# Turning z by overlapping twos of tiles, sixteen buffers of squares, shared homes for turned blocks and a changed plan, in a gated attention and token mixing kernel

## The chip, the cores and the metric

The kernel runs on one core of one Trainium2 chip. Its time is the device time of one execution in microseconds; lower is better. The figure for a kernel is the median of several runs. A profiled execution also has a span, from the first to the last instruction on the core; the device time holds that and a little around it.

## What is computed

There are 8 batches of 3200 tokens; u and v have 256 columns, z has 64. First a gated attention without a softmax, then a token mixer on its result:

```python
scores = scale * np.matmul(z, z.transpose(0, 2, 1))      # 3200 x 3200, symmetric
attn = np.maximum(scores, 0.0) ** 2
x = u * np.matmul(attn, v)

wq, wk = x @ w_q, x @ w_k                                # 64 columns each
W_tok = scale * np.einsum('bsd,btd->bst', wq, wk)
mixed = np.einsum('bst,btd->bsd', W_tok, x)
out = np.maximum(mixed, 0.0) @ w_out
```

The mixer is linear up to the maximum, so the kernel forms wk-transposed times x first (the "heads", 64 x 256) and never holds W_tok.

## The kernel before, in words

**Tiles and groups.** The 3200 tokens of a batch are 25 tiles of 128 rows. The columns of the score matrix are taken in 7 groups: six of 512 columns (four tiles) and one of 128. For a group `gi`, the product of the squared scores with v needs all 25 tiles of rows. Scores are symmetric, so a block of squares that was made in one group can be turned (transposed, by a DMA on SP's queue) and used in a later one: `is_turned` (L212) says that group `gi` makes for `gj` up to two groups further on (`FAR`, L45), and for the last group. So group 0 makes 25 tiles itself, group 1 makes 21, groups 2 to 5 make 17 each and the last one 1. Two such tiles make a pair; there are 460 or so pairs in all.

**A pair.** `scores` (L242) makes two tiles of scores on TensorE, with z turned (columns on partitions) as both operands. z has 64 columns, so the turned z of a batch, `zT`, holds it twice, on partitions 0 to 63 and on 64 to 127. One tile of the pair uses the top half of TensorE's rows, the other the bottom half, and the two run side by side. `first_stage` (L262) takes the maximum with zero and a scale out of PSUM, on ScalarE or VectorE. `second_stage` (L279) squares, on ScalarE or GpSimd, into an fp16 buffer `at` of the pool `pat` (`NAT`, 14 buffers, L52), and asks for the turning of what later groups need (`turn`, L304, into tiles `tt1`, `tt2` by the distance of the groups, or `ttl` for the last group).

**The second product.** `second_product` (L326) multiplies a tile of squares with v into four PSUM accumulators, two halves of the group by two halves of the rows; a group of 512 columns takes 100 steps of two matmuls. `gate` (L342) adds the two row halves (ScalarE copies, VectorE adds) and multiplies by u on GpSimd, which gives x in a buffer of `px` (`NX`, 6). x is turned by DMA (`turn_x`, L380, pool `pxt`, 3), projected to queries and keys (`projections`, L397), the keys are turned back and doubled (`turn_keys`, L416, `double_keys`, L426), and `heads` (L433) accumulates keys times x. When a batch's heads are known, `mix` (L462) and `proj` (L485) make the output rows, which SP stores.

**z of later batches.** `load_z` (L154) brings a batch's z in fp16 into a tile `zn` by a DMA of GpSimd's queue. `double_z` (L158) copies it twice by VectorE into `zd`, so that each token has its 64 values two times side by side. `turn_z` (L163) turns it in five DMAs of five tiles. Each turned block of 128 columns then has the same 64 values on the top and on the bottom partitions. z of the first batch is turned by TensorE instead (`turn_first`, L122), out of a buffer `zd0`.

**The order of the work.** The whole program is unrolled, and its order is written out by a planner that runs when the kernel is built (L556 to L997). It keeps a clock for each of TensorE, VectorE, ScalarE and GpSimd, adds a fixed cost for each instruction that it issues (`give`, L560), and holds lists of what may begin when: `later` (things at a time), `extras` (projections, heads, mixes, outputs), and `moves` (DMAs of SP, each with a time from which it is ready, a due time, an issue cost and a transfer cost; `move`, L581, `send`, L584). A transfer counts as landed `LANDS` (4.0) us after its cost. `row_at` tells from when a tile of squares may be used. The main loop (L963) takes, at each point of TensorE's clock, an extra, a pair of scores or a step of the second product. A pair counts as wanted when it stands in an even share of all pairs to all steps, 140 steps ahead (`lead`, L961); it can only be made when the pair `NAT` before it is used up and its turnings have landed:

```python
        wanted = able and p * total < (done_acc + lead) * NPAIR
```

What runs on the chip is the order that comes out; the engines wait for each other by semaphores, not by the planner's clock.

Of the kernel before, what the change touches and what calls it, by code (L numbers as in the profile page):

```python
# [16 lines left out]
def kernel(  # L17
# [34 lines left out]
    NAT = 14  # L52
    NX = 6
# [9 lines left out]
    pxt = ctx.enter_context(tc.tile_pool(name="pxt", bufs=3))  # L63
# [23 lines left out]
    zT, vs, us, xs, xTs, qks, ks, hacc, hss, rts, zds = ({} for _ in range(11))  # L87
# [64 lines left out]
    zdense, ztimes = {}, []  # L152

    def load_z(b):  # L154
        zdense[b] = pz.tile([P, NT, dqk], FP16, tag="zn", name="zn")
        nc.gpsimd.dma_start(out=zdense[b][:], in_=rows(z, b))

    def double_z(b, half):  # L158
        if half == 0:
            zds[b] = pz.tile([P, NT, 2, dqk], FP16, tag="zd", name="zd")  # L160
        nc.vector.tensor_copy(out=zds[b][:, :, half, :], in_=zdense[b][:])

    def turn_z(b, i):  # L163
        ztimes.append((b, i))
        if i == 0:
            zT[b] = pzt.tile([P, S], FP16, tag="zT2", name="zT2")
# [12 lines left out]
    wq32 = consts.tile([P, NC, dh], FP32, tag="wq32", name="wq32")  # L179
    wk32 = consts.tile([P, NC, dh], FP32, tag="wk32", name="wk32")  # L180
# [29 lines left out]
    SKIP = [(0, 2)]  # L210

    def is_turned(b, gi, gj):  # L212
        if b == 0 and (gi, gj) in SKIP:
            return False
        return gi < gj and (gj <= gi + FAR or gj == LASTG)
# [24 lines left out]
    made, turned = {}, {}  # L240

    def scores(p):  # L242
        assert len(ztimes) >= 5 * tiles[2 * p + 1][0] and p_chunk(p) in z_at, (p, clock, len(ztimes), z_at)
        sc = ps_tile("sc")
        for h, (b, gi, ti) in enumerate(tiles[2 * p : 2 * p + 2]):
# [3 lines left out]
                lhsT=zT[b][top(h), ts(ti, P)],  # L249
                rhs=zT[b][top(h), ds(gs, gw)],  # L250
# [28 lines left out]
    def second_stage(p, g, ways):  # L279
# [24 lines left out]
        def turn(b, gi, gj, n0, nn, c0, c1):  # L304
            if (b, gi, gj) not in turned:
                kind, nr, bufs = ("l", 1, 8) if gj == LASTG else (gj - gi, 4, gj - gi + 2)
                turned[b, gi, gj] = ptt.tile(
                    [P, nr, 4, P], FP16, tag=f"tt{kind}", name=f"tt{kind}", bufs=bufs
                )
# [32 lines left out]
    def gate(b, gi, half):  # L342
# [9 lines left out]
        if b == last and gi >= LASTG - 2:  # L352
            if gi == LASTG - 2 and half == 0:
                spare = pz.tile([P, NT, 2, dqk], FP16, tag="zd", name="xd")
                spare = spare[:].rearrange("p n a k -> p (n a k)")
                spare = spare[:, 0 : 9 * D].rearrange("p (n d) -> p n d", d=D)
# [23 lines left out]
    def turn_x(b, gi):  # L380
        assert len(xTs) < 3
# [192 lines left out]
    LANDS = 4.0  # L574
# [45 lines left out]

    SPLIT = 0.2
# [28 lines left out]
    def squares():  # L650
        while pending and pending[0][0] <= clock[PE] + 0.3:
# [9 lines left out]
            for (b, gi, gj, _, nn, _, _), turn in second_stage(p, g, ways):  # L661
                n = nn * widths[gi] // P
                due = done + (4.0 if gj == gi + 1 else 9.0)
                out_of[p] = out_of.get(p, 0) + 1
                move(done + SLACK, due + SLACK, 1.28, 0.21 * n, turn, lambda t, x=(p, b, gi, gj, nn): block_landed(t, *x))
# [17 lines left out]
    def use_keys(b, gi):  # L683
# [15 lines left out]
        if not final:  # L699
            move(  # L700
                done + SLACK, done + 10.0, 1.28, 0.21 * n, lambda: turn_keys(b, gi),
                lambda t: at_time(t, lambda: double(b, gi)),
            )
            keyed.append((b, gi))
# [46 lines left out]
    def use_proj(b, gi):  # L751
# [13 lines left out]
        move(done + SLACK, done + 6.0, 0.55, 1.6, stores[0], landed)  # L765
# [5 lines left out]
    Z0 = 24  # L771
    V0 = 56
    V1 = 11

    def batch_begun(b, t):
        if b + 1 < B:
            t0 = max(t + 6, Z0)
            at_time(t0, lambda: (load_z(b + 1), push(3.0)))
            for half in range(2):
                at_time(  # L780
                    t0 + 12 + 3 * half,
# [316 lines left out]
```

## Time and profile before

| | before |
|---|---|
| median of three runs | 784.41 us |
| the three runs | 782.69, 784.41 and 789.05 us |
| profiled execution | 784.44 us |
| its span | 782.7 us |
| granted TensorE clock | 0.999 |
| read from and written to HBM | 59.64 and 26.21 MB |

The profile gives, for each engine, the time in which it executed something (busy) and how many instructions that were. PE is TensorE with its matmuls, PEld its weight loads, DVE VectorE, ACT ScalarE, POOL GpSimd and SP the queue that issues most DMAs. "L332" is a line of the kernel. `acc` is the second product, `sc` the scores, `g` the result of the first stage, `at` the squares, `tt` and `ttl` turned blocks, `both` the sum of the row halves, `x_sb` x, `kx` the keys, `qk` queries and keys, `mx` and `fo` the output stage.

### The profile page before, as it was taken

What the parts mean: (1) busy time and instruction counts of PE and PEld (TensorE: products, weight loads), DVE (VectorE), ACT (ScalarE), POOL (GpSimd) and SP (SyncE); (2) the same over time, 40 slices, a digit from 0 to 9 for tenths busy, and PEclk for the clock granted to TensorE, in tenths of its full rate; (3) what the DMA queues carried; (4) which work ended last, traced back from release to release, by engine and by line L of the source; (5) the groups of instructions that cost most, each with busy time, mean ns of one, the idle gap of its engine ahead of it and who ended that gap; (6) DMA issues with size and microseconds to landing.
All of it is one profiled execution on the core that took longest, in us unless ns stands there. A gap on an engine that the chain in (4) does not pass through costs nothing.

```text
span 782.7 us, 28343 instructions
## 1 busy us (share of the span) xinstructions
PE 769.8 (98%) x12410; PEld 663.7 (85%) x12410; DVE 503.3 (64%) x515; ACT 546.4 (70%) x663; POOL 645.1 (82%) x530
## 2 busy tenths in 40 slices
PE   7999999999999999999999999999999999999996
PEld 5899999788899878888889887998889888898784
DVE  6766556655587556786476665777567556566635
ACT  6868777668676767766677767776678676777534
POOL 7898988788889877888789889778788879888961
PEclk9999999999999999999999999999999999999999
DMA  7999999999999999999799989999999998969635
GB/s 179 143 174 170 157 181 180 165 175 206 216 174 177 211 184 189 185 212 189 180 177 174 220 173 201 168 164 217 190 188 152 183 228 166 202 127 210 142 59 213
DMA packets 306300, 140.88 MB, mean 180 GB/s; under 512 B 285056, under 2 KB 287744, under 8 KB 306176
## 3 DMA queue, kind: packets, MB, share of 16 engines
q1 hardware_dynamic: 299408, 122.90, 82.1%
q0 software_dynamic: 6624, 15.98, 15.0%
q8 instruction: 97, 1.59, 0.9%
q10 hardware_dynamic: 144, 0.20, 0.1%
q14 instruction: 27, 0.22, 0.1%
HBM read 59.64 MB, written 26.21 MB: 110 GB/s over the span
## 4 chain that ended last, share of the span: by engine, by line
PE 92%; DVE 2%; DMA 1%; ACT 1%; POOL 1%; issue 1%; DVEq 0%; SPq 0%; ACTq 0%
PE acc L332 67%; PE sc L247 13%; PE fo L493 6%; PE qk L401 3%; PE qk L438 2%; PE mx L466 1%; DVE g L273 1%; DMA v_sb<-in_v_dram 1%; POOL at L291 1%; ACT g L269 1%; ACT at L289 0%; DMA z<-in_z_dram 0%; DVE fo L516 0%; PE hd L438 0%; DVE both L349 0%
## 5 line engine op out<-in xcount | busy, mean ns | idle before, releaser
L291 POOL TENSOR_TENSOR at<-g 128x1024 f16<-128x1024 f32 (+2 forms) x252 | 457.1, 1827 | 62.4 <-DVE g L273 50.3
L332 PE MATMUL acc<-v_sb,at 64*128 64x256 f16 x7344 | 498.4, 269 | 1.2 <-DMA v_sb<-in_v_dram 0.7
L273 DVE TENSOR_SCALAR g<-sc 128x1024 f32<-128x1024 f32 (+2 forms) x320 | 372.6, 1178 | 135.3 <-PE sc L247 126.7
L332 PEld LDWEIGHTS <-at 64*128 64x128 f16 x7344 | 400.9, 94 | 55.2 <-issue 8.1
L289 ACT ACTIVATE at<-g 128x1024 f16<-128x1024 f32 (+2 forms) x230 | 228.1, 1008 | 19.2 <-DVE g L273 17.0
L269 ACT ACTIVATE g<-sc 128x1024 f32<-128x1024 f32 (+2 forms) x159 | 156.5, 986 | 67.1 <-PE sc L247 58.5
L247 PE MATMUL sc<-zT 64*128 64x512 f16 x924 | 187.6, 377 | 1.9 <-DVE g L273 0.8
L370 POOL TENSOR_TENSOR x_sb<-both,u_sb 128x512 f16<-128x512 f32 (+1 forms) x112 | 134.7, 1209 | 43.9 <-DVE both L349 43.6
L332 PE MATMUL acc<-v_sb,tt 64*128 64x256 f16 x2272 | 159.2, 269 | 0.0
L332 PEld LDWEIGHTS <-tt 64*128 64x128 f16 x2272 | 123.5, 94 | 14.3
L349 DVE TENSOR_TENSOR both<-acc,both 128x512 f32<-128x512 f32 (+1 forms) x104 | 69.7, 670 | 86.4 <-ACT both L348 73.3
L348 ACT COPY both<-acc 128x512 f32<-128x512 f32 (+1 forms) x104 | 59.0, 568 | 70.7 <-PE acc L332 66.4
L247 PEld LDWEIGHTS <-zT 64*128 64x128 f16 x924 | 60.8, 94 | 12.9 <-issue 8.9
L521 ACT ACTIVATE fo<-fo 128x1024 f32<-128x1024 f32 (+1 forms) x48 | 44.6, 930 | 24.3 <-PE fo L493 23.8
L493 PE MATMUL fo<-wo,rt 128*128 128x256 f16 x400 | 53.2, 274 | 1.3 <-ACT rt L481 0.5
L483 ACT ACTIVATE rt<-mx 128x1024 f16<-128x1024 f32 (+1 forms) x49 | 45.6, 934 | 11.5 <-PE mx L466 11.2
L414 ACT CAST qk<-qk 128x512 f16<-128x512 f32 (+1 forms) x54 | 29.4, 544 | 30.0 <-PE qk L438 24.1
L493 PEld LDWEIGHTS <-rt 128*128 128x128 f16 x400 | 34.9, 98 | 15.8 <-issue 10.9
L453 DVE TENSOR_TENSOR ha<-qk,ha 128x512 f32<-128x512 f32 x37 | 25.6, 691 | 30.7 <-ACT qk L414 30.2
L401 PE MATMUL qk<-xT_sb,wqk 64*128 64x256 f16 (+1 forms) x404 | 32.4, 265 | 0.0
L431 POOL COPY kx<-kx 128x128 f16<-128x128 f16 (+1 forms) x99 | 26.2, 294 | 5.7 <-DMA kx<-qk 5.7
L438 PE MATMUL qk<-x_sb,kx 64*128 64x256 f16 x342 | 28.4, 269 | 0.0
(45 smaller groups left out, 233.7 us busy)
## 6 DMA issues: line engine op xcount, KB each, us to landing
u_sb<-in_u_dram SPq DMA_DIRECT2D x48, 512.0 KB, 4.9
out_dram<-fo SPq DMA_DIRECT2D x47, 512.0 KB, 5.2
v_sb<-in_v_dram POOLq DMA_DIRECT2D x35, 320.0 KB, 5.5
zn<-in_z_dram POOLq DMA_DIRECT2D x7, 400.0 KB, 6.8
tt<-at SPq DMA_TRANSPOSE x143, 4.3
u_sb<-in_u_dram SPq DMA_DIRECT2D x8, 128.0 KB, 3.1
out_dram<-fo SPq DMA_DIRECT2D x8, 128.0 KB, 3.4
xT_sb<-x_sb SPq DMA_TRANSPOSE x56, 5.8
```

What stands on the lines that cost most here:

```text
L247: nc.tensor.matmul(out=sc[:, h, 0:gw], lhsT=zT[b][top(h), ts(ti, P)], rhs=zT[b][top(h), ds(gs, gw)], start=True, stop=True,)
L269: nc.scalar.activation(out=g[:, hs, 0:w], in_=sc[:, hs, 0:w], func=RELU, scale=GSCALE)
L273: nc.vector.tensor_scalar(out=g[:, hs, 0:w], in0=sc[:, hs, 0:w], scalar1=0.0, scalar2=GSCALE, op0=AOP.max, op1=AOP.mult,)
L289: nc.scalar.square(out=out, in_=g[:, hs, 0:w])
L291: nc.gpsimd.tensor_mul(out=out, in0=g[:, hs, 0:w], in1=g[:, hs, 0:w])
L332: nc.tensor.matmul(out=accs[half, r][:, ds((j % 2) * D, D)], lhsT=weights(b, gi, ti, j)[top(r), :], rhs=vs[b][top(r), ti, :], start=(first ...
L348: nc.scalar.copy(out=both[:, 0 : n * D], in_=accs[half, 0][:, 0 : n * D])
L349: nc.vector.tensor_add(out=both[:, 0 : n * D], in0=accs[half, 1][:, 0 : n * D], in1=both[:, 0 : n * D])
L370: nc.gpsimd.tensor_mul(out=xs[b, gi][:, 0:n, :, r, :].rearrange("p n c d -> p (n c) d"), in0=both[:, 0 : n * D].rearrange("p (m d) -> p m ...
L401: nc.tensor.matmul(out=ps[:, r, 0 : n * P], lhsT=wqk[top(r), c, :, :].rearrange("p t h -> p (t h)"), rhs=xTs[b, gi][top(r), 0:n, c, :], st ...
L483: nc.scalar.activation(out=out, in_=ps[:, 0:nr, 0 : ND * n * P], func=RELU)
L493: nc.tensor.matmul(out=banks[r][:, ds(j * D, D)], lhsT=flat[:, ds((dc * n + j) * P, P)], rhs=wo[:, dc, :], start=(dc == 0 and j == 0), sto ...
```

## The change

- **z turned by overlapping twos of tiles.** `double_z` and its copies go, and with them `zd`. One tile `zn` holds all 25 tiles of z with one column of zeros (64 values) before and one behind. A turning takes two neighbouring tiles side by side as one block of 128 columns: block k of the turned z has tile k − 1 on the top partitions and tile k on the bottom ones. So `zT` is one block longer (26), and the top half is read 128 columns further on (`z_cols`), except for the first batch, which TensorE turns as before. The blocks are turned in four DMAs, even and odd ones apart, of 7, 7, 6 and 6 blocks, instead of five of 5.
- **Buffers.** 16 for squares (14), 7 for x (6), 4 for turned x (3). `zd0` and the spare tile of the last batch use buffers of v, the fp32 query and key weights use a buffer of the output stage.
- **Shared homes for turned blocks.** The seven buffers of `tt1` (3) and `tt2` (4) become seven homes for any block. A home is taken when the first turning of a block is sent and given back when the second product has used all rows of the block; a turning for which there is no home stays in the planner's list.
- **Pairs by need.** Each pair gets the step at which its own group wants it, spread evenly over that group's steps, and is wanted 140 steps ahead of it.
- **The plan's figures.** `LANDS` 8.0 (4.0), the cost of a turned block 0.17 (0.21), of rows of u or of the output 1.3 (1.6), of loads of z and v 2.2 and 1.8 (3.0 and 2.5); turnings for the last group from three groups off are due after 12 (9); the projections come 7 us after x has landed (3); z is turned from 14 us after its load on, in steps of 7 us (5 in the first batch), where it was 18 us and 6 (4).

`EXTRA` is empty and `STRETCH` is 1.0, so neither changes anything. The diff, cut to its core:

```diff
-    NAT = 14
-    NX = 6
+    NAT = 16
+    NX = 7
+    NXT = 4
...
-    zd0 = pz.tile([P, NT, 2, dqk], FP16, tag="zd", name="zd")
+    zd0 = pv.tile([P, NT, 2, dqk], FP16, tag="v_sb", name="zd")
...
-    zT[0] = pzt.tile([P, S], FP16, tag="zT2", name="zT2")
+    zT[0] = pzt.tile([P, S + P], FP16, tag="zT2", name="zT2")
+    zn = pz.tile([P, NT + 2, dqk], FP16, tag="zn", name="zn")
...
+    ZTURNS = [(0, 0, 7), (1, 0, 7), (0, 7, 13), (1, 7, 13)]
...
-    def double_z(b, half):
-        if half == 0:
-            zds[b] = pz.tile([P, NT, 2, dqk], FP16, tag="zd", name="zd")
-        nc.vector.tensor_copy(out=zds[b][:, :, half, :], in_=zdense[b][:])
...
         nc.sync.dma_start_transpose(
-            out=zT[b][:].rearrange("p (n s) -> p n s", s=P)[:, 5 * i : 5 * i + 5, :],
-            in_=zds[b][:, 5 * i : 5 * i + 5, :, :].rearrange("p n a k -> p (n a k)"),
+            out=zT[b][:].rearrange("p (m o s) -> p o m s", o=2, s=P)[:, odd, m0:m1, :],
+            in_=zn[:, 2 * m0 + odd : 2 * m1 + odd, :].rearrange("p n k -> p (n k)"),
         )
+
+    def z_cols(b, h, at, n):
+        return zT[b][top(h), ds(at + (P if b and h == 0 else 0), n)]
...
+    NHOME = 7
+    homes, homes_free = {}, list(range(NHOME))
+
+    def has_home(b, gi, gj):
+        return gj == LASTG or (b, gi, gj) in turned or bool(homes_free)
+
+    def give_home_back(b, gj, t):
+        gi = group_of(t)
+        if (b, gi, gj) in homes and all(
+            (b, gj, starts[gi] // P + n) in used for n in range(widths[gi] // P)
+        ):
+            homes_free.append(homes.pop((b, gi, gj)))
...
-                due = done + (4.0 if gj == gi + 1 else 9.0)
+                due = done + {1: 4.0, 2: 9.0}.get(gj - gi, FARDUE)
...
+                    lambda x=(b, gi, gj): has_home(*x),
...
-    LANDS = 4.0
+    LANDS = 8.0
+    BLOCK = 0.17
+    ROWS4 = 1.3
...
-    XWAIT = 3.0
+    XWAIT = 7.0
...
+    for p in range(NPAIR):
+        b, gi, _ = tiles[2 * p]
+        i0, i1 = first_of[b, gi], ends[b, gi]
+        n = NT * (widths[gi] // P)
+        need.append(steps[b, gi] + STRETCH * n * (2 * p - i0) / (i1 - i0))
...
-        wanted = able and p * total < (done_acc + lead) * NPAIR
+        wanted = able and need[p] < done_acc + lead
```

More of the change, by code (lines that the diff above doesn't have):

```diff
@@ L305, in turn @@
             if (b, gi, gj) not in turned:
[L306 to L309, printed above, removed]
+                if gj == LASTG:
+                    tag, nr, bufs = "ttl", 1, 8
+                else:
+                    homes[b, gi, gj] = home = homes_free.pop(0)
+                    tag, nr, bufs = f"tt{home}", 4, 1
+                turned[b, gi, gj] = ptt.tile([P, nr, 4, P], FP16, tag=tag, name=tag, bufs=bufs)
             out = turned[b, gi, gj][:].rearrange("p n j t -> p (n j) t")
@@ L777, in batch_begun @@
             t0 = max(t + 6, Z0)
[L778 to L781, printed above, removed]
-                    lambda half=half: (double_z(b + 1, half), give(DVE, clock[PE], 0.98)),
-                )
-            step = 6 if b else 4
-            for i in range(5):
+            if b == 0:
+                nc.gpsimd.memset(zn[:, 0 : NT + 2 : NT + 1, :], 0.0)
+            at_time(t0, lambda: (load_z(b + 1), push(2.2)))
+            step = ZSTEP if b else ZSTEP0
+            for i, (_, m0, m1) in enumerate(ZTURNS):
                 move(
-                    t0 + 18 + step * i, t0 + 34 + step * i, 1.28, 1.05,
+                    t0 + ZWAIT + step * i, t0 + ZDUE + step * i, 1.28, BLOCK * (m1 - m0),
                     lambda i=i: turn_z(b + 1, i),
@@ L903, in acc_step @@
         used.add(row)
+        if row:
+            give_home_back(*row)
         if closes:
@@ L961 @@
     lead = 140
+    STRETCH = 1.0
+    need, at, seen = [], 0, 0
+    steps = {}
+    for b in range(B):
+        for gi in range(NG):
+            steps[b, gi] = at
+            at += NT * (widths[gi] // P)
+    first_of = {}
+    for i, (b, gi, t) in enumerate(tiles):
+        first_of.setdefault((b, gi), i)
+    for p in range(NPAIR):
[3 more added lines that the diff above has]
+        need.append(steps[b, gi] + STRETCH * n * (2 * p - i0) / (i1 - i0))
     turn_about = False
```

57 lines of the change are left out of this document (32 added, 25 removed).

## The prediction

> **What bounds the kernel now.** I read the page's busy times first, then the chain that ended last, then busy times by stage, then who TensorE waited for.
>
> ```profile
> span 782.7 us, 28343 instructions
> PE 769.8 (98%) x12410; PEld 663.7 (85%) x12410; DVE 503.3 (64%) x515; ACT 546.4 (70%) x663; POOL 645.1 (82%) x530
> PE 92%; DVE 2%; DMA 1%; ACT 1%; POOL 1%; issue 1%; DVEq 0%; SPq 0%; ACTq 0%
> ```
>
> TensorE is busy for 98% and carries 92% of the chain. A busy TensorE need not be at its peak, because its matmuls overlap, so the pace has to be seen. The second view is the chain in order of time (start, us, what); its one long line is that of the stretch from 160 to 400 us alone.
>
> ```profile
> by line: PE acc L332 71.9%; PE sc L247 13.7%; PE fo L493 6.9%; PE qk L401 3.1%; PE qk L438 2.7%; PE mx L466 1.5%; PE hd L438 0.4%
> 252.45 1.85 PE fo L493 x16
> 254.95 1.86 PE acc L332 x34
> 740.76 0.22 PE sc L247 x2
> 747.84 11.79 PE acc L332 x214
> ```
>
> From 160 to 400 us the chain never leaves TensorE. The step of the second product takes 1.86/34 = 54.7 ns a matmul there, and 11.79/214 = 55.1 ns near the end, where there is nothing left but this step. So the pace is the same in the full kernel and with all other work gone: this is TensorE's own rate. Two matmuls run side by side, so a matmul shown as 269 ns long begins every 54.7 ns. Next, busy times by stage (stretch, its length, then TensorE matmuls, weight loads, VectorE, ScalarE, GpSimd with counts, granted clock, DMA share, GB/s):
>
> ```profile
> 0.00:20.00 20.00, 15.84 (x192) 11.88 (x194) 13.20 (x18) 12.28 (x20) 14.82 (x22) 1.00 0.75 177
> 20.00:40.00 20.00, 19.25 (x310) 16.61 (x308) 15.36 (x16) 16.71 (x22) 16.86 (x13) 1.00 0.93 142
> 40.00:60.00 20.00, 19.72 (x330) 18.19 (x327) 13.02 (x14) 14.21 (x18) 18.78 (x17) 1.00 1.12 179
> 80.00:120.00 40.00, 40.00 (x684) 38.85 (x682) 22.99 (x24) 31.41 (x40) 37.81 (x33) 1.00 1.20 161
> 120.00:140.00 20.00, 19.14 (x323) 17.12 (x321) 11.91 (x14) 14.54 (x17) 16.77 (x15) 1.00 1.00 173
> 160.00:760.00 600.00, 599.77 (x9774) 514.40 (x9770) 388.29 (x393) 417.56 (x498) 504.18 (x407) 1.00 0.98 183
> 760.00:783.00 23.00, 16.09 (x168) 11.19 (x163) 12.35 (x16) 9.91 (x19) 3.77 (x4) 0.97 0.49 183
> ```
>
> In 600 of the 782.7 us TensorE idles for 0.23 us. What idles is the start (4.16 us in the first 20), 0.75, 0.28 and 0.86 us in three stretches up to 140 us, and the end (22.7 − 16.09 = 6.6 us). What it waited for, by releaser (us in total, times, longest):
>
> ```profile
> PE hd L438 <- POOL kx L431: 0.9, 1, 0.9
> PE sc L247 <- DVE g L273: 0.8, 3, 0.4
> PE sc L247 <- ACT g L269: 0.8, 3, 0.3
> PE acc L332 <- DMA v_sb<-in_v_dram: 0.7, 1, 0.7
> PE acc L332 <- DVE both L349: 0.4, 2, 0.2
> ```
>
> Two rows for sizes below, a group of instructions (busy us, mean ns of one, idle before) and a step of the chain:
>
> ```profile
> L332 PE MATMUL acc<-v_sb,at 64*128 64x256 f16 x7344 | 498.4, 269 | 1.2 <-DMA v_sb<-in_v_dram 0.7 <-DVE both L349 0.4
> 138.51 0.28 PE hd L438 x2
> ```
>
> No row names a turned block, a turned z or a square's buffer. The changed kernel has the same number of matmuls in each product, so only these waits can give anything. The visible idle time from 20 to 760 us is 0.75 + 0.28 + 0.86 + 0.23 = 2.1 us. A gap shows short by up to 269 − 109 = 160 ns, because the last matmul before it is still running; with some eight gaps that is at most 1.3 us more: 3.4 us is all there is to gain there.
>
> The Trainium skill (Perfetto Trace Analysis, Identifying the Most-Contended Engine) says that matmul busy time is a poor measure of distance to the roofline and that the busy share of weight loads is a good one. By it, 85% would leave 119 us of headroom, and a change that hides waits could win far more than 1%. The equal paces above disagree: the weight loads are fewer per microsecond only where a matmul streams 512 columns.
>
> **The change part by part.** Counts of instructions in the changed kernel are from the order in which the two built programs hold them; no time is in it. Durations (groups first; then single instructions: start, us; then transfers: count and median us to landing) are these:
>
> ```profile
> L291 POOL TENSOR_TENSOR at<-g 128x1024 f16<-128x1024 f32 (+2 forms) x252 | 457.1, 1827 | 62.4 <-DVE g L273 50.3
> L273 DVE TENSOR_SCALAR g<-sc 128x1024 f32<-128x1024 f32 (+2 forms) x320 | 372.6, 1178 | 135.3 <-PE sc L247 126.7
> L289 ACT ACTIVATE at<-g 128x1024 f16<-128x1024 f32 (+2 forms) x230 | 228.1, 1008 | 19.2 <-DVE g L273 17.0
> L269 ACT ACTIVATE g<-sc 128x1024 f32<-128x1024 f32 (+2 forms) x159 | 156.5, 986 | 67.1 <-PE sc L247 58.5
> L161 DVE COPY zd<-zn 128x1600 f16<-128x1600 f16 x14 | 13.7, 975 | 0.0
> L291 POOL TENSOR_TENSOR at<-g 128x1024 f16<-128x1024 f32 x234 | 440.5, 1895 | 60.1 <-DVE g L273 48.5 <-issue 3.7 <-ACT g L269 3.0
> 40.04 0.97 DVE L161 COPY zd<-zn 128x1600 f16<-128x1600 f16 x1
> 310.83 1.91 POOL L291 TENSOR_TENSOR at<-g 128x1024 f16<-128x1024 f32 x1
> 311.32 0.98 DVE L161 COPY zd<-zn 128x1600 f16<-128x1600 f16 x1
> tt<-at SPq DMA_TRANSPOSE x143, 4.3
> zT<-zd SPq DMA_TRANSPOSE x35, 4.8
> ```
>
> *z without copies.* 14 copies of 975 ns leave VectorE: 13.7 us, none of it on the chain from 160 us on. The planner fills the room: 18 first stages move from ScalarE to VectorE and 18 squares from GpSimd to ScalarE. That is about +18 × 1.18 − 13.7 = +7.5 us on VectorE, +18 × (1.01 − 0.99) = +0.4 us on ScalarE, −18 × 1.895 = −34 us on GpSimd. All three stay below TensorE, so the cost and the gain are nothing beyond the waits above. Seven turnings of z per later batch in fives become four issues in sevens and sixes: 28 issues on SP for 35, 26 blocks a batch for 25. At 4.8 us for five blocks the extra block costs under 1 us of DMA per batch. What hides it: turned z is first read at a batch's end, and no row of TensorE waits names it; without that cover each issue would cost its 4.8 us. The two zero columns are one small memset on GpSimd's queue ahead of its first square, which waits there for its input anyway.
>
> The Trainium skill (SBUF — State Buffer, SBUF: two separate sides) says that a two-port VectorE copy locks GpSimd out of the shared port for its whole length. By it the 14 copies, the first at 40.04 us in the stretch where TensorE lost 0.28 us, would hold GpSimd for 13.7 us, and their removal could take that 0.28 us too: 782.8 us for my sum below. The trace disagrees: the square from 310.83 us runs beside the copy from 311.32 us and takes 1.91 us against a mean of 1.895 for its form, so I give nothing for it.
>
> *Sixteen buffers and pairs by need.* Pairs are now made ahead of the group that wants them instead of at an even rate. In matmuls of TensorE's order, the median distance from a pair's scores to the first use of its squares rises from 147 to 190 (5th percentile 93 to 89, least 67 to 53). At 54.7 ns, 147 matmuls are 8 us, 53 are 2.9 us, against about 1.2 + 1.8 us for the two stages by VectorE and GpSimd. So the typical cover grows, and the thinnest places are no safer than before.
>
> *Homes and late landings.* 141 two-tile turnings stand on SP as before. From the last scores that feed a turned block to its first use the median goes from 621 to 715 matmuls, 34 to 39 us, against 4.3 us for the transfer; the least is 313 matmuls (17 us), in the first batch. A transfer held back for a home waits in the planner's list, not on SP, so nothing queues behind it. Planning a landing at 8 instead of 4 us makes rows come into use later: this is the cover that grows. Nothing on TensorE waits for this now, so it brings nothing by itself; it removes a risk.
>
> *Buffers of x and turned x, shared weights and a spare.* Seven for six, four for three, three tiles moved into others' buffers: no instruction more. XWAIT of 7 moves the projections later, and the next batch's heads with them; no one waits for these at the seams, except once (0.9 us for `kx` at 138.5 us). The kernel's last stretch has the same instructions in nearly the same order.
>
> *What is added on TensorE.* 9 heads join a projection's tile instead of a tile of their own, but projections of the output stand alone two times more: 114 changes between 64-row and 128-row matmuls for 110. The row of 16 such matmuls takes 1.85 us, 16 × 109.4 ns would be 1.75, so a change costs about 0.1 us: +0.4 us. From below the bound is 0, if two changes of a visit cost it once, +0.2.
>
> *Sum.* The profiled execution took 784.44 us, its span 782.7, so 1.74 us lie around it; the median of the three runs is 784.41 (782.69 to 789.05). The waits from 20 to 760 us, 3.4 us at most, I take as half gone, because the order of the work is new from about 26 us on and brings waits of its own: −1.7. The changes of shape: +0.4. The start and the end, 4.16 + 6.6 us, keep their orders: 0. 784.44 − 1.7 + 0.4 = 783.1 us. Ends: all of the waits gone and shape changes at +0.2, 781.2; none gone, and as much again added, 784.44 + 3.4 + 0.4 = 788.2.
>
> **The rivals.**
>
> *The waits only move (no effect).* The rows allow it: they are few, each is a meeting of particular instructions, and the thinnest distances did not grow. 784.44 + 0.4 = 784.8 us.
>
> *Pairs by need crowd the first group of each batch (slower).* A pair costs (372.6 + 156.5 + 457.1 + 228.1)/462 = 2.63 us on three engines. Group 0 has 12.5 pairs in 100 steps of two matmuls, against 9.2 at an even rate. Its TensorE time is 200 × 0.0547 + 25 × 0.11 = 13.7 us and, with 1 to 2 us of heads and projections, some 15: 45 us on three engines. The pairs take 32.9, and the rest of the three engines' work, (503.3 + 546.4 + 645.1 − 1214.3)/50 = 9.6 us a group: 42.5 of 45, or 94%. If the engines fall behind in it, TensorE waits for squares at each batch's start. The stretch from 120 to 140 us shows the price: 0.86 us idle and up to three hidden 0.16 us, say 1.3. Seven batches: 9.1, so 784.44 + 9.1 + 0.4 = 793.9 us. It decides from 1.1 us a batch on. Against it: from 80 to 120 us GpSimd was busy 37.81 of 40 us, 95%, and TensorE idled for 0.00; and 16 buffers let pairs be spread over 140 steps.
>
> *All waits go, or more.* 784.44 − 3.4 + 0.2 = 781.2 us. For 1% (7.8 us) the start and end would have to shrink as well; the headroom that the weight loads' share suggests would be needed.
>
> **How the numbers follow.** Half of the waits gone: 0.50. They only move: 0.33. Crowded first groups: 0.11. All gone: 0.04; more than 1%: 0.02. The range takes in the first, second and fourth: from 781.2 less the scatter of the runs below their median (1.7) to the upper end 788.2 and a little for a run like the 789.05; 780 to 789 holds about 85%. A measurement of this kernel can tell about 1% from no change (below 776.6, above 792.3): faster 0.02, same 0.87, slower 0.11.
>
> **What would show it.** TensorE near 770 us busy, with its idle time from 160 to 760 us under 1 us, no wait of 0.9 us for `kx`, GpSimd near 611 us, VectorE near 511: right. Waits of `acc` for GpSimd or ScalarE squares once a batch: the crowding. A wait of `sc` for `zT`, or of `acc` for `tt`: the cover of z or the homes was misjudged. The prediction is wrong if the pace of 54.7 ns a matmul changes, or if an engine other than TensorE carries over 10% of the chain.

## The result, and the profile after

| | before | after |
|---|---|---|
| median of 21 runs | 785.17 us | 790.46 us |
| lowest to highest | 782.55 to 789.05 us | 784.74 to 796.50 us |
| ratio, with 95% interval | | 1.0064 (1.0041 to 1.0087) |
| profiled execution, span | 784.44, 782.7 us | 790.51, 788.7 us |

The changed kernel is slower by 0.6%, some 5 us, where 783.1 us was predicted; its runs also scatter more. The profiled execution lies at the median. The page of the profile after, its busy times and the chain that ended last by engine:

```profile
span 788.7 us, 28328 instructions
PE 770.9 (98%) x12410; PEld 662.6 (84%) x12410; DVE 506.8 (64%) x517; ACT 547.9 (69%) x661; POOL 615.5 (78%) x517
PE 91%; issue 2%; DVE 2%; POOL 2%; DMA 1%; ACT 1%; DVEq 0%; POOLq 0%; ACTq 0%
```

The sums say almost nothing: TensorE is still busy for 98% and the chain is still TensorE's. GpSimd lost 30 us of work, as the step on z said, and yet it is the engine that will turn out to be late. The busy times by stage show more (stretch, length, then TensorE matmuls, weight loads, VectorE, ScalarE, GpSimd with counts, granted clock, DMA share, GB/s):

```profile
0.00:20.00 20.00, 15.97 (x204) 12.59 (x205) 13.30 (x18) 12.92 (x22) 15.68 (x24) 1.00 0.76 183
20.00:40.00 20.00, 18.84 (x309) 16.50 (x304) 11.09 (x12) 14.10 (x20) 13.51 (x10) 1.00 0.86 148
160.00:240.00 80.00, 80.00 (x1327) 69.43 (x1323) 50.93 (x53) 59.82 (x71) 58.75 (x53) 1.00 0.98 175
240.00:280.00 40.00, 37.03 (x551) 29.63 (x549) 25.08 (x25) 23.46 (x27) 28.44 (x24) 0.96 1.04 201
280.00:320.00 40.00, 40.00 (x659) 32.75 (x655) 23.79 (x25) 26.45 (x31) 34.02 (x29) 1.00 1.04 170
320.00:360.00 40.00, 36.94 (x598) 31.35 (x595) 27.13 (x28) 26.91 (x32) 29.53 (x24) 1.00 1.09 153
360.00:760.00 400.00, 400.00 (x6538) 342.27 (x6536) 255.05 (x257) 280.51 (x335) 321.42 (x262) 1.00 0.98 183
760.00:789.00 29.00, 22.22 (x268) 16.29 (x264) 14.58 (x19) 12.10 (x22) 6.09 (x7) 0.97 0.45 169
```

The start idles 20 − 15.97 = 4.03 us (4.16 before) and the end 28.7 − 22.22 = 6.5 (6.6). From 160 to 760 us TensorE idles 6.03 us, where it had idled 0.23, and all of it lies in two places: 2.97 us between 240 and 280 us and 3.06 between 320 and 360. Over the whole span its idle time, span less busy time, went from 782.7 − 769.8 = 12.9 to 788.7 − 770.9 = 17.8 us. That is 4.9 us more, while the span grew by 6.0. The rest is busy time, and the column of the granted clock shows where to look: 0.96 between 240 and 280 us. Right behind the first place, the same view of a narrower stretch, then TensorE at the end of it and just after (start, us, instruction):

```profile
258.37:261.78 3.41, 3.41 (x36) 2.31 (x32) 2.45 (x2) 1.06 (x1) 3.39 (x4) 0.50 0.99 149
260.01 2.02 PE L352 MATMUL acc<-v_sb,at 64*128 64x256 f16 x18
262.08 1.04 PE L352 MATMUL acc<-v_sb,at 64*128 64x256 f16 x16
```

For 3.4 us the granted clock was half: 18 matmuls take 2.02 us there, where 16 take 1.04 us just after. As an estimate, half of the 3.4 us is lost, 1.7 us, which no idle time shows. In the kernel before, no stretch between 20 and 760 us has a clock under 1.00. So the two places, and the slow stretch behind the first, are the change in this execution. Who TensorE waited for (us in total, times, longest):

```profile
PE acc L352 <- POOL at L309: 2.6, 3, 1.2
PE hd L456 <- POOL kx L449: 1.4, 1, 1.4
PE mx L484 <- POOL hs L478: 1.3, 1, 1.3
PE qk L419 <- DMA xT_sb<-x_sb: 0.5, 1, 0.5
PE acc L352 <- DMA v_sb<-in_v_dram: 0.2, 1, 0.2
```

Instructions of GpSimd of three kinds are late: squares, the doubled keys, and a head's sum. Turned x, late by 0.5 us, comes on top in the first place. GpSimd is in order, so the question is what it stood before. This is the row of GpSimd's wait for the turned keys, first in the kernel before, then in the one after:

```profile
POOL kx L431 <- DMA kx<-qk: 5.7, 4, 2.0
```

```profile
POOL kx L449 <- DMA kx<-qk: 38.7, 10, 6.8
```

Four waits of 2.0 us at most became ten of up to 6.8, 38.7 us in total. The first of the two places shows how one of them gets to TensorE. GpSimd in order of time (start, us, engine, line, operation, output and input; in brackets the idle time before it and its releaser):

```profile
244.46 1.90 POOL L309 TENSOR_TENSOR at<-g 128x1024 f16<-128x1024 f32 x1 [0.56 <-DVE g L291]
253.16 0.53 POOL L449 COPY kx<-kx 128x128 f16<-128x128 f16 x2 [6.81 <-DMA kx<-qk]
253.65 3.75 POOL L309 TENSOR_TENSOR at<-g 128x1024 f16<-128x1024 f32 x2
```

GpSimd ends a square at 246.35 us and then stands for 6.81 us before two copies of keys that take 0.53 us together. Two squares wait behind the copies. The queue of SP in the same time:

```profile
238.64 2.50 SPq L402 DMA_TRANSPOSE xT_sb<-x_sb  x1
241.23 8.35 SPq L331 DMA_TRANSPOSE tt<-at  x4
249.67 1.61 SPq L437 DMA_TRANSPOSE kx<-qk  x1
251.37 1.22 SPq L331 DMA_TRANSPOSE ttl<-at  x1
```

The turning of the keys is issued at 249.67 us, behind four turnings of squares that took 8.35 us to issue. In the planner's own clock it was to start at 234.5 us and to be in use from 244.9. Laid beside the trace, with the scores on TensorE as the common ruler, that is 235.0 and 245.7 us. TensorE at the other end:

```profile
254.16 0.38 PE L265 MATMUL sc<-zT 64*128 64x512 f16 x2
255.60 0.61 PE L352 MATMUL acc<-v_sb,at 64*128 64x256 f16 x8 [1.07 <-POOL at L309]
257.46 0.72 PE L352 MATMUL acc<-v_sb,at 64*128 64x256 f16 x10 [1.24 <-POOL at L309]
```

It waits 1.07 and 1.24 us for the two squares that stood behind the copies. In the second place GpSimd waits 5.45 us for keys until 338.32 us, the heads wait 1.4 us for that copy, and a `mx` waits 1.3 us for a sum that GpSimd made a few instructions later.

**Two readings.** Theory A: the plan's lower figures for transfers make the planner put more on SP than SP can send, so SP runs behind the plan, the keys come late, GpSimd stands before their copy, and the squares behind it are late. The rival: the pairs by need, or the buffers, make a thinner order, and the wait for keys is only where it shows.

**What the row of DMAs does not show.** The profile's count, size and median us from issue to landing of the transfers after:

```profile
tt<-at SPq DMA_TRANSPOSE x143, 4.5
kx<-qk SPq DMA_TRANSPOSE x53, 4.4
```

Before, `tt` had 4.3, and `kx` this:

```profile
kx<-qk SPq DMA_TRANSPOSE x53, 4.1
```

From issue to landing hardly anything changed. A transfer that stands behind others on SP has not been issued yet, so this view starts its clock too late. The lateness has to be taken against the plan: how much later than planned SP started the turnings of the keys, by the common ruler above, for each kernel of this study:

| kernel | plan's figures | keys started late, mean and most | GpSimd waited for keys | ratio |
|---|---|---|---|---|
| before | old costs, landing 4 | −0.5, 3.3 us | 5.7 us | 1 |
| e4 | old costs, landing 4 | −1.2, 2.7 | 1.6 | 1.0002 |
| e7 | old costs, landing 4 | −0.7, 5.0 | 3.2 | 0.9996 |
| e12 | old costs, landing 4 | −0.6, 3.1 | no row | 0.9983 |
| e1 | old costs, landing 8 | −1.3, 3.8 | no row | 1.0399 |
| e11 | old costs, landing 8 | −0.6, 5.6 | no row | 1.0237 |
| e6 | low costs, landing 4 | 1.3, 7.1 | 23.0 | 1.0095 |
| e8 | low costs, landing 4 | 1.6, 12.1 | 58.9 | 1.0140 |
| e10 | low costs, landing 8 | 1.7, 10.0 | 26.7 | 1.0108 |
| e2 | low costs, landing 8 | 1.7, 9.6 | 21.4 | 1.0142 |
| e3 | low costs, landing 8 | 1.8, 10.5 | no row (its edit) | 1.0041 |
| e5 | low costs, landing 8 | 1.4, 9.7 | no row (its edit) | 1.0031 |
| e9 | low costs, landing 8 | 2.4, 11.2 | no row (its edit) | 1.0032 |
| after | low costs, landing 8 | 3.1, 14.6 | 38.7 | 1.0064 |

The ratio is of all runs; lateness and waits are of one profiled execution each, which is not always near the median. It took 786.78 us in e2 (the shortest of six), 784.99 in e3 (the third of 12), 801.83 in e8 (the second longest of six) and 787.28 in e10 (the second of six).

After, 15 of the 53 turnings of keys land later than the plan has them in use (5 of 53 before), and 53 of the 191 turnings of squares (18 before). VectorE, ScalarE and GpSimd otherwise keep the plan within 0.6 us on average. So it is the transfers that the plan holds for faster than they are. Its cost of an issue on SP, 1.28 us a turning, is the old one; the lowered figure is that of the transfer behind the issue, by which the plan holds SP back when transfers pile up.

### The profile page after: what moved, and what is told of

Read it like the earlier page. It is cut to its first block, busy times and chain, and to the rows that moved or that the text cites. A ratio compares the mean times of both kernels' runs of the same rounds, so it can differ in the third digit from the quotient of the medians.

```text
span 788.7 us, 28328 instructions
## 1 busy us (share of the span) xinstructions
PE 770.9 (98%) x12410; PEld 662.6 (84%) x12410; DVE 506.8 (64%) x517; ACT 547.9 (69%) x661; POOL 615.5 (78%) x517
## 4 chain that ended last, share of the span: by engine, by line
PE 91%; issue 2%; DVE 2%; POOL 2%; DMA 1%; ACT 1%; DVEq 0%; POOLq 0%; ACTq 0%
PE acc L352 65%; PE sc L265 13%; PE fo L511 6%; PE qk L419 3%; PE qk L456 2%; PE mx L484 1%; POOL at L309 1%; DVE g L291 1%; DMA v_sb<-in_v_dram 1%; ACT g L287 1%; DMA z<-in_z_dram 0%; ACT at L307 0%; DVE fo L534 0%; PE xtx L554 0%; DVE both L369 0%
## 5 line engine op out<-in xcount | busy, mean ns | idle before, releaser
L291 DVE TENSOR_SCALAR g<-sc 128x1024 f32<-128x1024 f32 (+2 forms) x336 | 390.3, 1185 | 122.6 <-PE sc L265 108.3
L309 POOL TENSOR_TENSOR at<-g 128x1024 f16<-128x1024 f32 (+2 forms) x238 | 426.2, 1803 | 44.8 <-DVE g L291 35.5
L307 ACT ACTIVATE at<-g 128x1024 f16<-128x1024 f32 (+2 forms) x244 | 245.3, 1020 | 12.9 <-DVE g L291 9.0
L265 PE MATMUL sc<-zT 64*128 64x512 f16 x924 | 190.7, 376 | 2.3 <-DVE g L291 1.0
L287 ACT ACTIVATE g<-sc 128x1024 f32<-128x1024 f32 (+1 forms) x143 | 138.8, 974 | 45.6 <-PE sc L265 41.0
L352 PE MATMUL acc<-v_sb,tt 64*128 64x256 f16 x2272 | 153.4, 269 | 0.0
L449 POOL COPY kx<-kx 128x128 f16<-128x128 f16 (+1 forms) x99 | 26.3, 295 | 38.9 <-DMA kx<-qk 38.7
L511 PEld LDWEIGHTS <-rt 128*128 128x128 f16 x400 | 34.8, 98 | 16.4 <-issue 11.2
```

Source lines behind the costliest of these rows:

```text
L265: nc.tensor.matmul(out=sc[:, h, 0:gw], lhsT=z_cols(b, h, ti * P, P), rhs=z_cols(b, h, gs, gw), start=True, stop=True,)
L287: nc.scalar.activation(out=g[:, hs, 0:w], in_=sc[:, hs, 0:w], func=RELU, scale=GSCALE)
L291: nc.vector.tensor_scalar(out=g[:, hs, 0:w], in0=sc[:, hs, 0:w], scalar1=0.0, scalar2=GSCALE, op0=AOP.max, op1=AOP.mult,)
L307: nc.scalar.square(out=out, in_=g[:, hs, 0:w])
L309: nc.gpsimd.tensor_mul(out=out, in0=g[:, hs, 0:w], in1=g[:, hs, 0:w])
L352: nc.tensor.matmul(out=accs[half, r][:, ds((j % 2) * D, D)], lhsT=weights(b, gi, ti, j)[top(r), :], rhs=vs[b][top(r), ti, :], start=(first ...
```

## The experiments

The ratios are against the kernel before, run alongside. Each time is a median of 5 to 12 runs.

### e1: the old costs in the kernel after

```diff
-    BLOCK = 0.17
-    ROWS4 = 1.3
+    BLOCK = 0.21
+    ROWS4 = 1.6
...
-            at_time(t0, lambda: (load_z(b + 1), push(2.2)))
+            at_time(t0, lambda: (load_z(b + 1), push(3.0)))
...
-        push(1.8)
+        push(2.5)
```

> The changed kernel with the plan's old transfer costs alone (a turned block 0.21 for 0.17, rows 1.6 for 1.3, loads of z and v 3.0 and 2.5 for 2.2 and 1.8). Theory A, the plan holds the DMA queue for faster than it is, so that SP falls up to 15 us behind the plan, the keys land late and GpSimd stands before their copy: SP again at most 5 us behind, GpSimd's wait for the keys under 10 us in total (38.7 before), 784 to 786 us. Theory B, pairs by need bunch the turnings at a batch's start whatever they are held to cost: SP still 10 us and more behind, over 25 us of GpSimd's wait, 788 to 791 us.

Measured: 814.79 us, ratio 1.0399 (1.0374 to 1.0424). SP is on time and no row has GpSimd waiting for keys, as theory A has it, and yet the kernel is 4% slower, which neither reading foresaw. Its waits:

```profile
PEld L265 <- issue: 24.1, 63, 1.7
PE sc L265 <- DVE g L291: 6.6, 14, 1.2
PE acc L352 <- DVE both L369: 3.8, 11, 0.5
```

TensorE waits for the stages of the scores and between the scores: the order now has stretches in which TensorE has nothing to do but the next pair. The planner's own clock for TensorE at the end of the main loop, in the plan and not on the chip, is 803.0 us here, 761.2 in the kernel after and 764.2 before, so the plan itself starves. With a landing at 8 us after an honest cost, rows come into use so late that the planner runs out of steps: this is argued from the plan, and e7 and e11 test it.

### e2: pairs at an even rate in the kernel after

```diff
-        wanted = able and need[p] < done_acc + lead
+        wanted = able and p * total < (done_acc + lead) * NPAIR
```

> The changed kernel with pairs wanted at the old even rate, all else as changed. Theory A: SP still 8 us and more behind the plan at places, GpSimd's wait for the keys over 15 us, 787 to 791 us. Theory B: SP at most 5 us behind, the wait under 10 us, 784 to 786 us.

Measured: 794.51 us, 1.0142 (1.0107 to 1.0176), more than either theory expected. Without pairs by need the kernel is slower, not faster, so they are not the cause. The wait is still there:

```profile
POOL kx L449 <- DMA kx<-qk: 21.4, 8, 5.6
```

In this execution, the shortest of six, it costs TensorE next to nothing: from 160 to 760 us TensorE idles 600 − 599.90 = 0.10 us, and its longest wait is one of 3.0 us for v at 110 us. What makes the other runs longer, this profile does not show.

### e3: the copy of the keys planned 8 us later in the kernel after

```diff
-                lambda t: at_time(t, lambda: double(b, gi)),
+                lambda t: at_time(t + 8.0, lambda: double(b, gi)),
```

> The changed kernel with the keys' copy placed 8 us later on GpSimd (and what uses it moved with it), transfers planned as changed. If the path from late transfers to TensorE runs through GpSimd standing before that copy (both theories): SP is as far behind as in the changed kernel, but GpSimd waits for the keys under 10 us and TensorE has no wait for squares of 1 us; 785 to 787 us. If TensorE waits for late turned blocks or late x instead: no faster than 789 us, with waits of TensorE for DMAs.

Measured: 786.76 us, 1.0041 (1.0013 to 1.0070). SP is still up to 10.5 us behind on the keys, but GpSimd no longer stands before the copy. The main part and the end of this kernel (span 783.2 us), then of the one after (788.7 us):

```profile
40.00:740.00 700.00, 699.56 (x11475) 606.31 (x11476) 449.46 (x454) 510.18 (x602) 584.39 (x475) 1.00 1.04 183
740.00:800.00 60.00, 33.19 (x434) 25.08 (x428) 16.40 (x22) 18.03 (x30) 8.81 (x12) 0.96 0.31 111
```

```profile
40.00:740.00 700.00, 693.83 (x11311) 599.52 (x11312) 458.43 (x457) 498.76 (x586) 570.05 (x470) 1.00 1.03 182
740.00:789.00 49.00, 42.22 (x598) 33.94 (x592) 23.95 (x31) 22.16 (x37) 16.29 (x15) 0.98 0.44 149
```

In the main part TensorE idles 0.44 us instead of 6.17. GpSimd's squares end at most 0.4 us behind the plan, where in the kernel after they end up to 6.0 us behind. So for these two executions the way from the late keys through GpSimd to TensorE is shown: with the keys still up to 10.5 us late and GpSimd not standing, the main part loses nothing. The whole time gains less, because the keys of the last batch are planned later too: from 740 us to the end TensorE idles 43.2 − 33.19 = 10.0 us instead of 48.7 − 42.22 = 6.5. The median is 3.7 us below that of the kernel after, but each has its own runs of the kernel before: by the ratios, 1.0041 against 1.0064, some 2 us come back, and the two intervals overlap. This execution is one of the shorter ones (784.51 to 795.26 us). So how much of the loss in the median goes by this way is not settled.

### e4: pairs by need alone in the kernel before

```diff
-        wanted = able and p * total < (done_acc + lead) * NPAIR
+        wanted = able and need[p] < done_acc + lead
```

> The kernel before with pairs by need alone. Theory A, in which the old costs keep the transfers apart: SP at most 5 us behind the plan, 784 to 786 us. Theory B: SP 10 us and more behind, GpSimd waiting for keys or TensorE for squares at each batch's start, 788 us and more.

Measured: 784.25 us, 1.0002 (0.9975 to 1.0030). Pairs by need neither help nor harm by themselves. With e2 this closes the rival for the pairs.

### e5: as e3, the last batch left as it was

```diff
+                lambda t: at_time(t + (8.0 if b < last else 0.0), lambda: double(b, gi)),
```

> The changed kernel with the keys' copy 8 us later on GpSimd in all batches but the last, where the delay itself lay on the path. If GpSimd standing before that copy is the whole loss: GpSimd waits for keys under 10 us, TensorE loses under 1.5 us from 40 to 760 us, 782.5 to 784.5 us, no slower than the kernel before. If late transfers also hold TensorE by other ways: 786 us and more.

Measured: 787.65 us, 1.0031 (0.9997 to 1.0064), by the expectation the case in which late transfers hold TensorE by other ways too. There are six runs from 783.7 to 785.9 us and six from 789.4 to 792.1. No row has GpSimd waiting for keys. The profiled execution is one of the long ones, 792.14 us, and shows another transfer late:

```profile
PE acc L352 <- DMA v_sb<-in_v_dram: 5.4, 2, 4.1
```

A load of v was issued on GpSimd's queue at 104.33 us and took 11.5 us to land; the longest wait is 4.1 us. From 116.2 us on, at the end of that wait, the granted clock was half for 3.4 us, as in the kernel after. With the keys out of the way, v is what comes late here.

### e6: the low costs in the kernel before

```diff
-                move(done + SLACK, due + SLACK, 1.28, 0.21 * n, turn, ...
+                move(done + SLACK, due + SLACK, 1.28, 0.17 * n, turn, ...
-        move(done + SLACK, done + 6.0, 0.55, 1.6, stores[0], landed)
+        move(done + SLACK, done + 6.0, 0.55, 1.3, stores[0], landed)
...
```

The same for the turnings of keys and x, the loads of u, z (3.0 to 2.2; its turnings 1.05 to 0.85) and v (2.5 to 1.8).

> The kernel before with the plan's new, lower transfer costs alone (a turned block 0.17, rows 1.3, loads 2.2 and 1.8; landings still 4 us). Theory A: the lower costs alone put SP 8 us and more behind the plan and GpSimd before the keys for over 20 us: 788 to 795 us, more than the changed kernel, since landings are not planned late. Theory C, that the lower costs are harmless and it is the turning of z or the homes: 784 to 785 us, SP at most 5 us behind.

Measured: 792.39 us, 1.0095 (1.0065 to 1.0125). The low costs alone make the kernel before as slow as the kernel after or slower. GpSimd waits for the keys again, but no row of TensorE's matmuls names the doubled keys or GpSimd's squares. What TensorE waits for most is turned x that lands late:

```profile
POOL kx L431 <- DMA kx<-qk: 23.0, 15, 4.6
PE qk L401 <- DMA xT_sb<-x_sb: 4.7, 3, 2.0
```

### e7: the kernel after with the old costs and the old landing

The edit of e1, and

```diff
-    LANDS = 8.0
+    LANDS = 4.0
```

> The changed kernel with the old transfer costs and landings after 4 us, so that the turning of z, the buffers, the homes and pairs by need are left with the old plan. Theory A: SP at most 5 us behind, GpSimd's wait for keys under 10 us, 782.5 to 785 us. Theory C: SP 8 us and more behind at places, 788 us and more.

Measured: 785.31 us, 0.9996 (0.9970 to 1.0021). All of the rest of the change is in this kernel: z without copies, 16 buffers, homes, pairs by need, the later projections. Its wait for keys and its main part:

```profile
POOL kx L449 <- DMA kx<-qk: 3.2, 3, 1.6
160.00:760.00 600.00, 599.13 (x9752) 510.58 (x9748) 369.07 (x375) 428.64 (x511) 493.67 (x400) 1.00 1.03 183
```

TensorE idles 0.87 us in 600. So the loss of the change lies in the plan's costs of transfers and its landing, and the rest is worth nothing that can be measured (the interval is 0.3% to either side).

### e8: the kernel after with the old landing and the low costs

```diff
-    LANDS = 8.0
+    LANDS = 4.0
```

> The changed kernel with landings planned after 4 us and its low costs kept. Theory A: SP as far behind as in the changed kernel (10 us and more), and with less allowance for it the keys' copies stand earlier on GpSimd, which waits over 50 us for them: 793 us and more. Theory D, that late landings crowd the transfers: SP less far behind, 784 to 787 us.

Measured: 793.70 us, 1.0140 (1.0082 to 1.0198). The wait for keys is the longest of all, and the heads wait for the copy:

```profile
POOL kx L449 <- DMA kx<-qk: 58.9, 15, 10.4
PE qk L456 <- POOL kx L449: 7.8, 2, 7.3
```

This execution is one of two long ones (801.83 and 803.34 us, the other four 792.73 to 793.83), so the size of its waits is not that of the median. By the medians the time grows without the late landing, though the interval touches that of the kernel after: in the changed kernel the late landing looks like a cushion for the low costs.

### e9: as e5, and v loaded earlier

```diff
-    V0 = 56
-    V1 = 11
+    V0 = 48
+    V1 = 10
```

> As the kernel with the keys' copy later in all batches but the last, and v of the second batch loaded from 48 us on in steps of 10 (it was 56 and 11). If the slow half of that kernel's runs (789 to 792 us against 784 to 786) comes from the last load of v landing late at the second batch's start: TensorE has no wait of over 1 us for v at 100 to 120 us, 783.5 to 785.5 us, and no run above 788. If the scatter has another source: runs on both sides as before, median 786 to 788 us.

Measured: 786.01 us, 1.0032 (1.0013 to 1.0052); four of 12 runs still lie from 788 to 791 us. The waits for v are 1.2 us in the profiled execution, but that is one of the short ones (785.11 us), and the ratio is that of e5. v was late in the long execution of e5 that was profiled; why the other long runs are long stays open.

### e10: the low costs and the late landing in the kernel before

The edit of e6 and `LANDS = 8.0`.

> The kernel before with the lower transfer costs and landings after 8 us. If late landing is what makes up for the low costs: SP still 5 to 10 us behind the plan, but TensorE waits for no transfer of over 1 us; 785 to 788 us, faster than with the low costs alone (792). If it does not: 790 us and more.

Measured: 792.68 us, 1.0108 (1.0070 to 1.0145), where less was expected. The late landing does not make up for the low costs here:

```profile
POOL kx L431 <- DMA kx<-qk: 26.7, 9, 5.6
```

SP is up to 10.0 us behind on the keys, more than with a landing at 4 us (7.1). So a landing at 8 us gives nothing back in the kernel before; why the two kernels differ was not tried. In this execution, a short one, TensorE idles 2.0 us from 160 to 760 us, and no row has it waiting for keys.

### e11: the late landing alone in the kernel before

```diff
-    LANDS = 4.0
+    LANDS = 8.0
```

> The kernel before with landings after 8 us alone, costs as they were. The run with the old costs in the changed kernel took 814.8 us with SP on time, which no theory had: the reading is that late landings and honest costs together leave the planner without rows, so that it writes an order that stands still by itself. By that: SP at most 4 us behind, no waits of GpSimd for keys, and TensorE with waits for VectorE and ScalarE between scores that follow each other; 795 to 815 us. If not, 784 to 788 us.

Measured: 802.53 us, 1.0237 (1.0213 to 1.0262), with no wait for keys:

```profile
PE sc L247 <- DVE g L273: 5.3, 11, 1.1
```

SP is at most 5.6 us behind, a little over the 4 expected. This is what e1 showed, in the kernel before: the old costs and a landing planned too late make an order that stands still by itself (the plan's clock for TensorE ends its main loop at 789.2 us, against 764.2).

### e12: as e7, with the copy of the keys 3 us later

```diff
-                lambda t: at_time(t, lambda: double(b, gi)),
+                lambda t: at_time(t + (3.0 if b < last else 0.0), lambda: double(b, gi)),
```

> The changed kernel with the old costs and landings after 4 us, and the keys' copy 3 us later on GpSimd in all batches but the last. A version with everything that the runs favour: 783 to 785 us, at most 0.3% faster than the kernel before, since TensorE has only 1 to 3 us of waits from 40 to 760 us to lose.

Measured: 783.34 us, 0.9983 (0.9962 to 1.0004). The lowest median of the study, but the interval reaches 1: not shown to beat the kernel before. Its main part idles 0.29 us, no less than that of the kernel before (0.23):

```profile
160.00:760.00 600.00, 599.71 (x9781) 512.12 (x9778) 368.33 (x374) 433.61 (x516) 489.45 (x400) 1.00 1.00 183
```

## Why the prediction was wrong, step by step

**Right.** TensorE is the bound, and from 160 to 760 us it is busy without a gap away from the two places, at the old pace but for the 3.4 us at half clock. z without copies brought nothing and moved the work as said: GpSimd 615.5 us (about 611), VectorE 506.8 (about 511), and no row of TensorE's waits names `zT`. The homes hold nobody up: no row names `tt`. Pairs by need do not crowd a batch's start (e4: 1.0002). The buffers and homes cost nothing that can be measured (e7: 0.9996).

**Wrong: "Homes and late landings", and with it "no one waits for these".** The step that failed is the one that took the plan's figures for a matter of cover. It took the late landing for something that "brings nothing by itself" and "removes a risk", and it left the lower costs of transfers out of the sum, at nothing and without a reason, though the list of the change has them. Put alone into the kernel before, the lower costs cost 0.95% (e6) and the late landing 2.4% (e11); with both taken back, the changed kernel loses nothing (e7). What the lower costs do is crowd SP: turnings are sent faster than they are passed on, keys start up to 14.6 us late, and the order of the plan no longer fits. The sentence that a transfer held back waits in the list, "so nothing queues behind it", looks at the homes; four turnings of squares that the planner did send stood in front of the keys.

The second half of the failure is where it looked. It checked the distance from a turned block to its first use by TensorE, 34 to 39 us, and that cover held. The late transfer was another one, the keys, whose reader is a copy of 0.27 us on GpSimd with squares queued behind it. The profile of before had the warning in a row that the prediction quoted as 0.9 us that might go: TensorE's `hd` waiting for GpSimd's `kx`. One step further back stood GpSimd's own 5.7 us for the keys, the largest wait for a transfer in that profile, by an engine that makes squares for TensorE right behind it. A low busy share is no cover for that: GpSimd was less busy after (78%) than before (82%).

**The sum.** The waits from 20 to 760 us were to give −1.7 us. The idle time there grew by 5.2 us instead, from 2.1 to 7.3: 2.97 + 3.06 us in the two places, where the old order had no gap, less 0.6 us before 160 us. The half clock behind the first place adds an estimated 1.7 us, for which the sum had no term. The changes of shape, the start and the end stayed within a few tenths. The upper end of the range, "none gone, and as much again added", had the kind of case right and was still too low, since it took the size of new waits from the old ones (3.4 us) and not from the row that could grow, a standing GpSimd.

**Two smaller points.** The "seven turnings of z per later batch" are five in each of seven batches, 35 in the row of transfers; the count of 28 for 35 is right. Of the copy beside the square at 310.83 us: the square had begun first, so this pair can't show a square held up by a copy. It shows that the copy wasn't held up either, 0.98 us against a mean of 975 ns. The mean of a full square on GpSimd is 1895 ns in both profiles, with the copies and without them. Whether this copy is of the two-port kind is not shown.

**The rivals.** The time, 790.46 us, lies between that of waits that only move (784.8) and that of the crowding rival (793.9), but it did not come by the crowding: with the even rate back in the kernel after the time is 1.0142, and the waits of `acc` for squares are three in the whole kernel, two of them in one place, and not one a batch. Of the list of what would show it, the wait for `kx` was the one that spoke: it grew to 1.4 us, and behind it lay 38.7.

**The Trainium skill's busy share of weight loads** (Perfetto Trace Analysis, Identifying the Most-Contended Engine), by which 85% would leave room, is no guide here either. In e3's main part weight loads are busy for 606.31 of 700 us, 87%, with TensorE idle for 0.44 us; in the kernel after for 599.52, 86%, with 6.17 us idle. The difference of one point is real, but the level says nothing of room: at 87% there was nothing left to gain. The measurement decides, and the idle time by stage is what tells.

**Open.** Which of the lowered costs (turned blocks, rows, loads) does the harm was not tried apart. That low costs make transfers late and the kernel slow is shown by whole runs; by which transfer the time is lost differs between the profiled executions: squares behind the keys in the kernel after, turned x in e6, the heads before the keys in e8, v in e2 and e5. With the keys' copy moved away the kernel is still 0.3 to 0.4% above the kernel before by its ratios (e3, e5, e9); the profiles put it at the end of the kernel and at late v, but the scatter of their runs is explained only in part. Loss and lateness don't go in proportion: e6 is up to 7.1 us behind and loses 0.95%, the kernel after 14.6 us and 0.64%; whether what stands behind a late transfer is soon used may decide, and that is a matter of the order; it was not tried.

## What to carry to other kernels

A planner's cost for a transfer is a promise about a queue. Set a little too low, 0.17 us a block for 0.21, it let the queue fall up to 14.6 us behind the plan, and whichever engine stands before a late transfer passes the delay on to what is queued behind: GpSimd before the keys here, TensorE before turned x in e6. So price a change of a plan's figures like any other step, with the question which engine stands before a transfer and what is queued behind that instruction; a busy share of 78% does not answer it. Cost and landing margin belong together: the higher costs with a landing at 4 us lose nothing here, the low costs lose 0.6 to 1.4% with either landing (0.3 to 0.4% with the keys' copy moved), and the higher costs with the late landing lose 2 to 4%.

## What the runs showed of the hardware that was not expected

- The time to issue a turning of squares (`tt`) isn't fixed. In the kernel after, the 131 that began within 0.2 us of the issue before them took 1.21 to 6.80 us, with a median of 1.33; the five that began after SP had idled for 1 us or more took 1.23 to 1.31. The four of 241.23 us took 8.35 us, 2.1 us each on average.
- SP's total time of issuing up to 760 us was the same, some 615 us before and 612 after. Nearly the same work in another order made a backlog of up to 14.6 us.
- The median time from issue to landing stayed at 4.1 to 4.5 us in a kernel whose transfers were up to 14.6 us late: that view is blind to a queue.
- The changed order has the wider scatter: 21 runs from 784.74 to 796.50 us, half of them between 787.3 and 792.5, beside 782.55 to 789.05 for the kernel before, half between 783.0 and 786.4. Beside the experiments the kernel before had single runs up to 793.74 us.
- Behind some longer waits of TensorE the granted clock is halved for a while, and the wait then costs more than its length. Stretches of half granted clock, each of 3.4 us, begin at 258.4 us in the kernel after (behind waits of 1.07 and 1.24 us), at 112.7 in e2 (in a wait of 3.0 us) and at 116.2 in e5 (after one of 4.1 us); in e8 one of 6.8 us begins at 81.1 us (in a wait of 7.3 us). Not every such wait has one: in e6 a wait of 2.0 us at 611.6 us has none, and the second place of the kernel after, with 1.4 and 1.3 us, has none.
